# Running W2 and Wo of three chunks as eight 32x64 lanes that also carry the next chunk's attention

## The chip, the cores and the metric

The kernel runs on one core of one Trainium2 chip. The metric is the device time of one execution in microseconds (us). Matrix products run on TensorE (PE), which takes a weight load and a matmul as two instructions; VectorE (DVE), ScalarE (ACT) and GpSimd (POOL) do the elementwise work, and the sequencers of SyncE (SP) and ScalarE issue the DMAs. Each engine works through its own list of instructions in order; semaphores tie the lists together.

## The reference

For 2048 tokens of width 576, in bf16:

```python
xn  = layernorm(x)
out = x + attention(xn, wqkv, wo) + swiglu(xn, w1, w3, w2)

# attention: 32 heads of 18 columns, a causal window of 256 tokens
scores = q @ k.T * 18 ** -0.5
mask   = (i - j >= 0) & (i - j < 256)
o      = softmax(where(mask, scores, -1e9)) @ v
# swiglu: 4608 hidden columns
h      = silu(xn @ w1) * (xn @ w3)
y      = h @ w2
```

## The kernel before

The tokens go through in four **chunks** of 512 (`CH`). A chunk has three stages on PE, one after the other.

**Projection** (`proj_begin`, `proj_end`, `proj_part`; matmuls on line 445): nine items, `("q", 0..3)` and `("8", 7)` for queries and keys and `("v", 0..3)` for values, in the order of `PROJ`. Each item fills a pair of PSUM banks in two halves, and the halves of neighbouring items alternate. DVE and ACT copy queries and keys to SBUF tiles `stage[:, 0..8, :]`. There a head's 18 rows stand at the wrong partitions, so DMAs from SBUF to SBUF move them into `qv` and `kv` (`span_main`, line 512; `span_last`, lines 541 and 543). These DMAs are issued by SP, some by ACT.

**Units** (line 697): 36 units of 18 matmuls (64 rows, 128 columns of weights, 512 tokens streamed; two of them, on the upper and the lower 64 rows, run side by side). A unit makes 128 hidden columns: ACT's tanh (line 706) and two DVE operations (lines 712 and 715) write `hT`. The chunk's attention is threaded between the units, and for later chunks also between the projection's items: `spaced_step` places a **score step** (line 571) when the loop's counter `clock` says so. A score step takes four heads: two 64-row tiles, each with two heads in block-diagonal keys. ACT takes the exponential (line 580), POOL masks (line 607). When all steps of eight heads (`j`, four such groups) are masked, `pv` (line 628) multiplies with the values in eight tiles of 64 rows by 32 columns, and `pv_out`, `o_scale`, `o_turn` and `o_pack` (DVE transposes on lines 637 and 650, reciprocals on 642, a POOL multiplication on 643, DMAs on 654) normalise the result and move it to `oT`. The fourth `pv` comes after the units; its transposes run beside W2.

**W2 and Wo** (`p2_list`, `p2_item`; lines 757, 763, 683): for two halves of 288 output columns, 36 blocks of hidden columns times four token tiles, each a full 128x128 tile with 288 columns streamed; then Wo; DVE adds `x` (line 770) and SP stores the result (line 772). W2's weights come in tiles of four blocks, 288 KB each, into four slots (`load_w2`, line 345); a slot is loaded again when its last use has been placed.

The order of all lists is written out by the loop at the end of the kernel: what it adds first stands first in its engine's list. `_Prog.add` notes who wrote and who read each buffer, and `resolve` turns that into semaphore waits. `job()` hands out three bank pairs in turn for projection items and units, so a unit's matmuls wait until DVE is done with the unit three before it. `load_part` (line 318) brings W1 and W3 in parts of 192 KB.

Of the kernel before, what the change touches and what calls it, by code (L numbers as in the profile page):

```python
# [164 lines left out]
def bass_parallel_sum__sliding_block__glu_gated_swiglu__prompt_kernel(  # L165
# [32 lines left out]
    with ExitStack() as es:  # L198
# [4 lines left out]
        NXP, NOF, NPT, NW13, NW2, NOD = 7, 4, 10, 3, 4, 2  # L203
# [17 lines left out]
        w2 = [sb(f"w2_{i}", [128, 4, HD]) for i in range(NW2)]  # L221
        hT = sb("hT", [128, NF, CH])
        stage = sb("stage", [128, 9, CH])
        qv = sb("qv", [128, G, CH])
        kv = sb("kv", [128, G, NB, 2 * KB])
        kb4 = sb("kb4", [128, G, NV - NB, 2 * KB])
        va = sb("va", [128, NV, G, 2, VW])
# [30 lines left out]
        oT = sb("oT", [128, 5, CH])  # L258
        th = [sb(f"th{i}", [128, CH]) for i in range(2)]
        gs = [sb(f"gs{i}", [128, CH]) for i in range(2)]  # L260
# [77 lines left out]
        def load_w2():  # L338
            nonlocal n2fill
            if n2fill >= NC * 2 * NFC:  # L340
                return
            s = n2fill % NW2
            half, fc = divmod(n2fill % (2 * NFC), NFC)
            n2fill += 1
            add("sp", lambda e: e.dma_start(
                w2[s][:], B_w2[fc * 512:(fc + 1) * 512, half * HD:(half + 1) * HD].rearrange("(fl p) d -> p fl d", p=128)),
                w=[("w2", s)], dma=f"w2_{s}")
# [70 lines left out]
        def pair_of(c, i):  # L418

            return (((0, 1), (2, 3), (8, 4), (5, 6)) if c == 0 else ((8, 0), (1, 2), (3, 4), (5, 6)))[i]  # L420
# [68 lines left out]
        def v_evac(c, tt, b, r, eng):  # L489
            pos = (c * NB + 2 * tt + r) % NV  # L490
            for p in range(2):
                src = PS[64 * r:64 * r + 64, b:b + 2, 0:HD].rearrange("p b (n e d) -> p e b n d", e=2, d=Dh)[:, p, :, :, :]
                dst = va[64 * p:64 * p + 64, pos, :, :, 0:Dh].rearrange("p (b g) n d -> p b (g n) d", b=2)
                kw = {"j" if p else "w": [("va", pos)]}
                if eng == "act":
                    add("act", lambda e, dst=dst, src=src: e.activation(dst, src, ACT.Copy), r=[("ps", b), ("ps", b + 1)], **kw)
                else:
                    add("dve", lambda e, dst=dst, src=src: e.tensor_copy(dst, src), r=[("ps", b), ("ps", b + 1)], **kw)

        def keys_of(a, b, p0, n, p):  # L500
            return kv[p0:p0 + n, a:b, :, KB * p:KB * p + KB].rearrange("q g b f -> q (g b) f")

        SPREAD = 3

        def span_issue(a, b, moves, first, only=slice(None)):
            seen = set()
            for n, (kind, eng, tset, dst, src) in enumerate(moves):
                if n not in range(len(moves))[only]:
                    seen.add(kind)
                    continue  # L510
                keys = [(kind, g) for g in range(a, b)]
                add(eng, lambda e, dst=dst, src=src: e.dma_start(dst, src), r=st_keys(*tset), dma=f"{kind}_{a}",
                    **{"j" if kind in seen or not first else "w": keys})
                seen.add(kind)

        def span_main(a, b, q_eng="sp", only=slice(None)):

            gs_ = list(range(a, b))
            moves = []
            for pr in range(2):  # L520
                moves.append(("q", q_eng, gs_, qv[64 * pr:64 * pr + 2 * Dh, a:b, :], stage[2 * Dh * pr:2 * Dh * (pr + 1), a:b, :]))
            for i in range(3):
                r0 = 4 * Dh + i * Dh
                moves.append(("k", "sp", gs_, keys_of(a, b, 64 * (i // 2) + Dh * (i % 2), Dh, i % 2),
                              stage[r0:r0 + Dh, a:b, :].rearrange("q g (b f) -> q (g b) f", f=KB)))
            span_issue(a, b, moves, True, only)

        def span_last(a, b, only=slice(None)):

            p0 = 64 + Dh  # L530
            order = sorted(range(a, b), key=lambda g: g == SPREAD and a != 2)
            for g in order[only]:
                r0 = (g - (g > SPREAD)) * Dh
                moves = [("k", "sp", [8], keys_of(g, g + 1, p0, Dh, 1),
                          stage[r0:r0 + Dh, 8, :].rearrange("q (b f) -> q b f", f=KB))]
                if g == SPREAD:
                    moves = [("k", "sp", range(9), kv[p0 + r:p0 + r + 2 * 9 - 1:2, g, :, KB:2 * KB], stage[126 + r:127 + r, :, :])
                             for r in range(2)]
                for kind, eng, tset, dst, src in moves:
                    if a == 2:  # L540
                        add(eng, lambda e, dst=dst, src=src: e.dma_start(dst, src), r=st_keys(*tset), j=[("k", g)], dma=f"kl_{g}")
                    else:
                        add(eng, lambda e, dst=dst, src=src: e.dma_start(dst, src), r=st_keys(*tset),
                            j=[("k", x) for x in range(a, b)], dma=f"k_{a}")

        def repack_span(a, b, q_eng="sp"):
            span_main(a, b, q_eng)
            span_last(a, b)

        def keep_keys(g):  # L550
            add("pool", lambda e: e.tensor_copy(
                kb4[:, g, :, :].bitcast(dt.float32), kv[:, g, 2 * NB - NV:NB, :].bitcast(dt.float32)),
                r=[("k", g)], w=[("kp", g)])
# [11 lines left out]
        def scores(c, g, s):  # L565
            col = 0
            for n, (kb, q0, nb) in enumerate(steps_of(c)[s]):
                for r in range(2):
                    r0 = 64 * r
                    out_ = PS[:, SC[r], col * KB:(col + nb) * KB]  # L570
                    add("pe", lambda e, r0=r0, out_=out_, kb=kb, q0=q0, nb=nb: e.matmul(  # L571
                        out_, kb4[r0:r0 + 64, g, kb + NV - NB, :] if kb < 0 else kv[r0:r0 + 64, g, kb, :], qv[r0:r0 + 64, g, q0 * KB:(q0 + nb) * KB],
                        start=True, stop=True, tile_position=(r0, 0)),
                        r=[("kp" if kb < 0 else "k", g), ("q", g)], **{"j" if n else "w": [("ps", SC[r])]})
                col += nb

        def exps(c, g, s, sl):
            pt_of[(c, g, s)] = sl
            w = KB * sum(nb for _, _, nb in steps_of(c)[s])
            add("act", lambda e: e.activation(  # L580
                pt_slot(sl)[:, 0:w, :], PS[:, SC[0]:SC[1] + 1, 0:w].rearrange("p r q -> p q r"), ACT.Exp, scale=scale),
                r=[("ps", b) for b in SC], w=pt_keys(sl))

        def masks(c, g, s):

            at = []
# [8 lines left out]
            sl = pt_of[(c, g, s)]  # L595
# [14 lines left out]
        def pv(c, j, banks):  # L610
# [4 lines left out]
            for s, st in enumerate(steps_of(c)):  # L615
                col = 0
                for kb, q0, nb in st:
                    n += 1
                    pos = (c * NB + kb) % NV
                    for gi in range(2):  # L620
                        g = 2 * j + gi
                        sl = pt_of[(c, g, s)]
                        for pr in range(2):
                            for p in range(2):
# [493 lines left out]
```

## Time and profile before

| | |
|---|---|
| median of 3 runs | 559.48 us (559.39 to 560.43) |
| span of the profiled execution | 557.7 us |
| median less span | 1.8 us |
| PE busy, share of the chain that ended last | 553.1 us (99%), 98% |
| a chunk's period (projection start to projection start) | 137.5 us (142.44 to 279.94 to 417.44) |
| one W2 and Wo stage, chunk 1 | 39.56 us (240.21 to 279.77) |
| a unit of 18 matmuls | 1.94 us |
| ACT, DVE, POOL busy | 259.4, 309.6, 163.3 us |

The profile shows one execution. In its tables of groups, "out<-in" names the tensors, then stands the shape and how often it ran; times are busy us, mean ns of one, and the engine's idle time ahead of it. A timeline row gives the start and the length of a merged run of instructions. An instruction of SP or ACT that issues a DMA is listed under "SPq" or "ACTq", with the time for which that sequencer was held by it; "to landing" is the time from issue to the last of its data.

### The profile page before, as it was taken

To read this page: it belongs to the slowest core of one execution; us is meant where nothing else is said; L and a number is where in the kernel's file an instruction comes from. 1 tells how busy PE (TensorE), PEld (TensorE's weight loads), DVE (VectorE), ACT (ScalarE), POOL (GpSimd) and SP (SyncE) were. 2 spreads that over 40 slices of the span, in tenths; PEclk is the share of its full clock that TensorE was granted. 3 is DMA by queue.
4 is the path that set the end of the run, shared out by engine and by line. 5 is a ranking of instruction groups with operands and counts; after the bars stand their busy time and mean duration, and the time that the engine had idled before them with its cause. 6 is when DMAs were issued, how large, how long until landed. Compare 5 with 4: busy or idle time off the path is not lost.

```text
span 557.7 us, 15727 instructions
## 1 busy us (share of the span) xinstructions
PE 553.1 (99%) x6766; PEld 332.9 (60%) x6766; DVE 309.6 (56%) x578; ACT 259.4 (47%) x357; POOL 163.3 (29%) x389
## 2 busy tenths in 40 slices
PE   8999999999999999999999999999999999999998
PEld 4445545787655455477764554548776555455776
DVE  6465889610365778851056668884105577777211
ACT  6457776100387776500048777650005776765000
POOL 5513454300034445330003444423001343432000
PEclk9999999999999999999999999999999999999999
DMA  9987989978576358466956744966593673562552
GB/s 234 228 177 179 207 141 196 165 201 225 135 139 146 110 139 188 125 144 174 238 107 139 166 115 113 182 153 140 151 249 78 135 172 98 129 142 54 139 149 65
DMA packets 127072, 85.96 MB, mean 154 GB/s; under 512 B 34179, under 2 KB 124763, under 8 KB 127003
## 3 DMA queue, kind: packets, MB, share of 16 engines
q1 hardware_dynamic: 125011, 82.69, 64.5%
q10 hardware_dynamic: 1992, 2.27, 1.7%
q8 instruction: 53, 0.87, 0.7%
q14 instruction: 16, 0.13, 0.1%
HBM read 71.29 MB, written 2.36 MB: 132 GB/s over the span
## 4 chain that ended last, share of the span: by engine, by line
PE 98%; DMA 1%; DVE 0%; ACT 0%; issue 0%; POOL 0%
PE ps L697 50%; PE ps L757 25%; PE ps L445 9%; PE ps L571 6%; PE ps L628 4%; PE ps L763 3%; DMA xp<-in_A_x_dram 1%; PE ps L683 0%; PE ps L390 0%; DVE xn L370 0%; ACT stage L825 0%; ACT xnT L397 0%; DVE stats L353 0%; DVE ofin L770 0%; POOL xn L373 0%
## 5 line engine op out<-in xcount | busy, mean ns | idle before, releaser
L697 PE MATMUL ps<-xnT,w 64*128 64x512 bf16 x1400 | 182.9, 376 | 0.0
L697 PE MATMUL ps<-xnS,w 64*128 64x512 bf16 x1120 | 150.9, 376 | 0.0
L757 PE MATMUL ps<-w,hT 128*128 128x288 bf16 x1152 | 146.6, 286 | 0.0
L712 DVE SCALAR_TENSOR_TENSOR gs<-th,ps 128x512 bf16<-128x512 bf16 x144 | 98.0, 681 | 81.4 <-ACT th L706 80.8
L580 ACT ACTIVATE pt<-ps 128x1024 bf16<-128x1024 f32 (+1 forms) x112 | 113.2, 1010 | 53.5 <-PE ps L571 53.0
L757 PEld LDWEIGHTS ps<-w,hT 128*128 128x128 bf16 x1152 | 112.3, 98 | 29.0 <-issue 0.2
L607 POOL TENSOR_TENSOR pt<-pt,mk 128x128 int32<-128x128 int32 (+1 forms) x199 | 80.8, 428 | 79.2 <-ACT pt L580 79.2
L697 PEld LDWEIGHTS ps<-xnT,w 64*128 64x128 bf16 x1400 | 66.5, 94 | 62.8 <-issue 0.3
L706 ACT ACTIVATE th<-ps 128x512 bf16<-128x512 f32 x144 | 85.5, 594 | 35.3 <-PE ps L697 34.7
L715 DVE SCALAR_TENSOR_TENSOR hT<-gs,ps 128x512 bf16<-128x512 bf16 x144 | 98.9, 687 | 4.9
L697 PEld LDWEIGHTS ps<-xnS,w 64*128 64x128 bf16 x1120 | 53.8, 94 | 54.3
L770 DVE TENSOR_TENSOR ofin<-ps,xp 128x288 bf16<-128x288 f32 x32 | 13.8, 455 | 124.9 <-PE ps L763 66.8
L458 ACT ACTIVATE stage<-ps 128x512 bf16<-128x512 f32 x16 | 9.5, 596 | 142.0 <-PE ps L445 139.7
L607 POOL TENSOR_TENSOR hT<-hT,mk 128x128 int32<-128x128 int32 (+1 forms) x31 | 12.4, 422 | 164.3 <-ACT hT L580 164.3
L571 PE MATMUL ps<-qv,kv 64*128 64x320 bf16 (+4 forms) x528 | 51.5, 260 | 0.0
L571 PEld LDWEIGHTS ps<-qv,kv 64*128 64x128 bf16 x528 | 25.3, 94 | 28.1 <-ACT hT L580 1.7
L445 PE MATMUL ps<-xnT,wp 64*128 64x512 bf16 (+1 forms) x360 | 37.9, 355 | 0.0
L650 DVE STREAM_TRANSPOSE od<-oq 128x256 bf16<-128x256 bf16 x64 | 25.8, 427 | 7.0 <-POOL oq L643 7.0
L580 ACT ACTIVATE stage<-ps 128x1024 bf16<-128x1024 f32 x24 | 24.6, 1024 | 10.2 <-PE ps L571 10.0
L445 PEld LDWEIGHTS ps<-xnT,wp 64*128 64x128 bf16 x360 | 18.9, 94 | 14.5
L643 POOL TENSOR_TENSOR oq<-uq,rden 128x288 bf16<-128x288 f32 x16 | 10.8, 673 | 40.7 <-DVE rden L642 40.7
L445 PE MATMUL ps<-wv,xnT 64*128 64x288 bf16 x288 | 22.2, 283 | 0.1
(75 smaller groups left out, 345.4 us busy)
## 6 DMA issues: line engine op xcount, KB each, us to landing
w<-in_B_w_dram SPq DMA_DIRECT2D x208, 192.0 KB, 4.2
w<-in_B_w_dram SPq DMA_DIRECT2D x72, 288.0 KB, 3.4
xp<-in_A_x_dram SPq DMA_DIRECT2D x30, 144.0 KB, 3.5
out_dram<-ofin SPq DMA_DIRECT2D x32, 72.0 KB, 2.0
xnS<-xnT SPq DMA_DIRECT2D x8, 256.0 KB, 6.6
oT<-od SPq DMA_DIRECT2D x40, 36.0 KB
pt<-in_A_wqkv_dram SPq DMA_DIRECT2D x4, 288.0 KB, 6.8
hT<-in_B_w_dram SPq DMA_DIRECT2D x6, 192.0 KB, 4.2
```

What stands on the lines that cost most here:

```text
L445: op = add("pe", lambda e, out_=out_, st=st, mv=mv, n=n, r0=r0, first=first: e.matmul(out_, st, mv, start=first, stop=(part == 1 and n == ...
L571: add("pe", lambda e, r0=r0, out_=out_, kb=kb, q0=q0, nb=nb: e.matmul(out_, kb4[r0:r0 + 64, g, kb + NV - NB, :] if kb < 0 else kv[r0:r0 + ...
L580: add("act", lambda e: e.activation(pt_slot(sl)[:, 0:w, :], PS[:, SC[0]:SC[1] + 1, 0:w].rearrange("p r q -> p q r"), ACT.Exp, scale=scale) ...
L607: add("pool", lambda e, vb=vb, mm=mm: e.tensor_tensor(vb, vb, mm, ALU.mult), r=(key if n == 0 else []) + ["mk"], **{"w" if n == 0 else "j" ...
L628: add("pe", lambda e, p=p, q=q, pr=pr, sl=sl, g=g, pos=pos, q0=q0, nb=nb, col=col, first=first, n=n: e.matmul(PS[32 * q:32 * q + VW, banks ...
L650: add("dve", lambda e: e.transpose(od[i][:, g % 2, c0:c0 + CH // 2], oq[:, c0:c0 + CH // 2]), r=["oq", "oq0"], **{"j" if half or g % 2 els ...
L697: op = add("pe", lambda e, n=n, r0=r0, r=r, k=k, src=src: e.matmul(PS[:, b0 + r, :], wt[r0:r0 + 64, k, fl * 128:(fl + 1) * 128], src, star ...
L706: add("act", lambda e: e.activation(th[i][:], PS[:, bg, :], ACT.Tanh, scale=0.5), r=[("ps", bg)], w=[("th", i)])
L712: add("dve", lambda e: e.scalar_tensor_tensor(out=gs[i][:], in0=th[i][:], scalar=1.0, in1=PS[:, bg, :], op0=ALU.add, op1=ALU.mult), r=[("t ...
L715: add("dve", lambda e: e.scalar_tensor_tensor(out=hT[:, u, :], in0=gs[i][:], scalar=0.5, in1=PS[:, bu, :], op0=ALU.mult, op1=ALU.mult), r= ...
L757: add("pe", lambda e: e.matmul(bank, hT[:, f, tt * 128:(tt + 1) * 128], w2[sl][:, k, :], start=(f == 0 and half == 1), stop=False), r=[("h ...
L763: add("pe", lambda e: e.matmul(bank, oT[:, k, tt * 128:(tt + 1) * 128], wo[:, k, d0:d0 + HD], start=False, stop=(k == 3 and (half == 0 or ...
```

## The change

**The attention of chunks 1 to 3 moves.** It no longer runs between units: chunk c+1 is projected right after chunk c's units, and its scores and PVs run inside chunk c's W2 and Wo stage. Chunk 0's attention stays between chunk 0's units; chunk 3's W2 stays as it was, apart from the size of the tiles.

**W2 and Wo of chunks 0 to 2 run in eight lanes.** A lane is one of 4 x 2 tiles of 32 rows by 64 columns. For one half, a token tile's 36 blocks are split over four row groups; each group adds into another token tile's bank, and the groups change banks in eight stages (`TURNS`). A stage that takes over a bank waits, through a semaphore (`after`), until the last owner's matmul has ended. A lane has 18 matmuls of W2 in a stage, and Wo's in between.

**Scores take eight heads.** Four lanes do one step of heads (`h2` 0 or 1) while the other four go on with W2. Queries and keys therefore stand at eight places of 18 rows, each on a 32-row border, and are moved there by more DMAs (`spans`). The planner in `w2_lanes` keeps a clock for each lane and writes the matmuls of all lanes, the exponentials, masks, PVs and `events` (loads of W1 and W3, `x`, `xn_swap`, the steps behind a PV) in one order. Scores use two bank pairs in turn.

**W2's tiles** are six blocks (432 KB) in five slots. Their memory also holds chunk 0's keys (`kz`), so chunk 0's tiles are loaded from the hooks of chunk 1's projection.

```diff
-        NXP, NOF, NPT, NW13, NW2, NOD = 7, 4, 10, 3, 4, 2
+        NXP, NOF, NPT, NW13, NW2, NOD = 7, 4, 10, 3, 5, 2
+        FT = 6
-            return (((0, 1), (2, 3), (8, 4), (5, 6)) if c == 0 else ((8, 0), (1, 2), (3, 4), (5, 6)))[i]
+            return (((0, 1), (2, 3), (8, 4), (5, 6)) if c == 0 else ((8, 0), (4, 1), (5, 2), (6, 3)))[i]
...
+        def span(c, kind, hd, half, a, b, eng="sp"):
+            h2, r = divmod(hd, 2)
+            row = 64 * r + 32 * (half ^ h2)
+            rows = slice(row, row + Dh)
...
+            if kind == "q":
+                moves.append((range(a, b), ts, qv[rows, h2, a:b, :], stage[Dh * hd:Dh * hd + Dh, tile_, :]))
+            elif hd < 3:
+                src = stage[4 * Dh + hd * Dh:5 * Dh + hd * Dh, tile_, :]
...
+                    if c % 2 == 0:
+                        moves.append((range(a, b), ts, kq[rows, h2, a:b, 0:2, :].rearrange("q g c f -> q g (c f)"), src))
+                    else:
+                        moves += [(range(a, b), ts, kq[rows, h2, a:b, 2 * x, :], src[:, :, 4 * KB * x:4 * KB * x + 4 * KB]) for x in range(2)]
...
+        def spans(c, a, b):
+            for hd in range(4):
+                for half in range(2):
+                    span(c, "q", hd, half, a, b, "act" if hd > 1 else "sp")
+                for half in range(2):
+                    span(c, "k", hd, half, a, b)
...
+        def score_ops(c, unit, bank):
+            j, h2, s = unit
...
+                            lane = (2 * r + (half ^ h2), half)
+                            rows, at = slice(32 * lane[0], 32 * lane[0] + Dh), (32 * lane[0], 64 * half)
+                            out_, st = PS[64 * half:64 * half + 64, bank[r], cols], kd[rows, h2, j, key_at(c, kb), :]
...
+                                r=[("k", j), ("q", j)], **kw)
...
+        TURNS = ((0, 2, 3, 1), (1, 3, 2, 0), (2, 0, 1, 3), (3, 1, 0, 2))
+        LANES = [(a, b) for a in range(4) for b in range(2)]
...
+        def lane_matmul(c, half, lane, t, k, first, after):
+            a, b = lane
+            rows = slice(32 * a, 32 * a + 32)
+            toks = slice(t * 128 + 64 * b, t * 128 + 64 * b + 64)
...
+                st, mv, keys = hT[rows, i, toks], w2[sl][rows, i % FT, :], [("h", i), ("w2", sl)]
...
+            out_ = PS[64 * b:64 * b + 64, ACC[t], 0:HD]
+            return add("pe", lambda e: e.matmul(
+                out_, st, mv, start=first == "w" or first == "s", stop=False,
+                tile_position=(32 * a, 64 * b), skip_group_check=True),
+                r=keys, after=after, **{"w" if first == "w" else "j": [("ps", ACC[t])]})
...
+                elif head and stage_ != 4:
+                    known = [v[1] for key_, v in ended.items() if key_[:2] == (half, stage_ - 1)]
+                    after = (max(known, key=lambda o: o.pos),)
...
+                if k[0] == "w2":
+                    i = half * NT2 + k[1] // FT
+                    uses[i] = uses.get(i, 0) + 1
+                    if uses[i] == 8 * 4 * FT:
+                        load_w2(c)
+            while events:
+                events.pop(0)[1]()
...
-                    span_main(2, G, "act", slice(2, None))
-                if c == 0 and u == 2:
-                    span_last(2, G, slice(0, 1))
+                    for hd in range(3):
+                        for half in range(2):
+                            span(0, "k", hd, half, 0, 4)
+                if c == 0 and u in (2, 3, 4, 5):
+                    for half in range(2):
+                        span(0, "k", 3, half, u - 2, u - 1)
...
+                if c and u in (25, 27, 29, 31, 33):
+                    load_w2(c)
...
+                hooks = {("q", 2): [lambda: spans(c + 1, 0, 2)], ("8", 7): [lambda: spans(c + 1, 2, 4)]}
+                if c == 0:
...
+                    pv(c, 3, banks)
...
+                    for what in (("q", 0), ("v", 0), ("v", 1), ("v", 2), ("v", 3)):
+                        hooks.setdefault(what, []).append(lambda: load_w2(0, first))
...
+                project(c + 1, hooks)
+                two = (job_ctr - 1) % 3
+                ACC[:] = [*JOBS[(two + 1) % 3], *JOBS[(two + 2) % 3]]
...
+                events = [(3000 + 3200 * i, lambda: parts(1)) for i in range(12)]
...
+                w2_lanes(c, xs, [SC, JOBS[two]], events, put_pv, 1500)
```

## The prediction

> **What bounds the kernel now.** I read the page's busy times and its chain of work first, then the timelines of PE and of SP, then single lines.
>
> ```profile
> PE 553.1 (99%) x6766; PEld 332.9 (60%) x6766; DVE 309.6 (56%) x578; ACT 259.4 (47%) x357; POOL 163.3 (29%) x389
> PE 98%; DMA 1%; DVE 0%; ACT 0%; issue 0%; POOL 0%
> ```
>
> PE is the bound from end to end. So PE time that goes is gained in full, and every wait that PE's list now meets is paid in full. Chunk 2's projection in the timeline of SP's sequencer:
>
> ```profile
> 283.61 2.59 SPq L512 DMA_DIRECT2D kv<-stage  x3
> 286.25 0.77 SPq L543 DMA_DIRECT2D kv<-stage  x1
> 287.12 1.59 SPq L512 DMA_DIRECT2D qv<-stage  x2
> 288.75 2.47 SPq L512 DMA_DIRECT2D kv<-stage  x3
> 291.26 1.59 SPq L543 DMA_DIRECT2D kv<-stage  x2
> 292.89 1.38 SPq L318 DMA_DIRECT2D w<-in_B_w_dram  x2
> ```
>
> Eleven moves of queries and keys follow each other from 283.61 to 292.89: SP is held 0.84 us by each. The line views give the same whatever the size, and a W2 tile holds SP half as long:
>
> ```profile
> L512 SPq DMA_DIRECT2D kv<-stage x33: 781/813/3058, 17.9 to 437.9; - x33
> L543 SPq DMA_DIRECT2D kv<-stage x29: 764/782/1378, 20.6 to 444.3; - x29
> L345 SPq DMA_DIRECT2D w<-in_B_w_dram x18: 368/388/552, 242.4 to 279.1; - x18
> ```
>
> Today these moves are spread: the first score needs six of them, four on SP. That list is what I hold the change against.
>
> **PE's own work, per moved chunk.** A score step costs a unit 0.22 us (a unit start every 1.94 us, 2.16 with a step); 40 steps a chunk are 8.8 us. In lanes a step streams the same 512 columns, but on four of eight lanes: 4.4 us of every lane. That removes 4.4 us. W2 and Wo: 320 matmuls in 39.56 us, 122.5 ns each; a lane has 324 (288 + 32 + 4), so 39.7 us if eight run side by side. The trace has no 32x64 tile. Its nearest row is PV, eight 64x32 tiles:
>
> ```profile
> 53.05 0.32 PE L628 MATMUL ps<-hT,va 64*20 64x320 bf16 x4
> 53.06 0.32 PE L628 MATMUL ps<-pt,va 64*20 64x320 bf16 x4
> 53.19 0.25 PE L628 MATMUL ps<-hT,va 64*20 64x192 bf16 x4
> ```
>
> Eight matmuls of 320 columns take 0.14 us, as one does at the units' rate (512 in 0.216). Upper bound: weight loads come in turn. PV's densest loads are 24 of 20 columns in 0.2 us from 514.67, 8.3 ns each; if that is the price of the columns, 64 cost 27 ns and a round of eight lanes 0.213 us instead of 0.1225: +29 us a chunk. But PV's early groups start eight tiles at once, loads included, so I take 39.7.
>
> The Trainium skill, "TensorE: Matmul & The Clock Gate", section "Wait — 56ns, not 53.3ns?", speaks against the change: matmul starts never come closer than about 25 ns, so eight lanes would need 200 ns a round. By it the three stages would be 75 us longer. The trace does not bear it out: seven PV matmuls of 64 columns start from 53.48 to 53.52.
>
> Handing over banks: a 288-column matmul lasts 286 ns and its slot 122, so its result comes some 0.2 us after the slot's end. Twelve hand-overs are 2.4 us, and between the halves a lane waits for up to four DVE adds of 455 ns, 0.9 on average: 3.3 us, 0 if scores fill them all. I take 3.5 with the lanes' unequal ends before a PV. PVs cost the same in both kernels; switches of tile shape are two a chunk in both. Net −0.9 a chunk, **−2.7 us** for three (ends −13 and +3).
>
> **The key moves.** In the changed order the first score of chunk c+1 stands behind 18 matmuls of each lane, 2.2 us into the lanes, and waits for all queries and keys of the first `spans` call: 14 DMAs on SP for chunk 2, 20 for chunks 1 and 3, plus four on ACT. PE's list is in order, so W2 of all lanes stands behind that score. Time from the projection's start: bare projection 13.0 (13.4 from 142.44 to 155.87, less two steps), lanes from 13.2, score due at 15.4. SP can do the first move early; its second needs item ("q", 2), which PE ends at 7.55 (287.3 less 279.77), plus 0.2 and DVE's 0.69: 8.5. The call's last move is for the next group of heads and isn't needed. Landing takes 2.4 to 3.0 from the issue in oT's rows; I take 2.4.
>
> - Chunk 2: 14 less the first and the last are 12, so the last needed starts at 8.5 + 11 x 0.84 = 17.7 and lands at 20.1: PE waits **4.7**. Behind them SP has the second call (15), then two W1/W3 parts (0.65 each), and only then the load of W2's sixth tile, whose slot the first tile held: issued at 19.4 (the first call's end, 8.5 + 13 x 0.84) + 12.6 + 1.3 = 33.3. A 288 KB tile lands in 3.3 us (3.0 to 6.5); 432 KB I put at 4.0 (3.3 to 5.0, in proportion): 37.3. PE wants it after 88.5 matmuls a lane, 1.2 of scores and 0.7 of hand-overs, lane time 12.7: 20.1 + 10.5 = 30.6. Wait **6.7**.
> - Chunk 3: 18 moves, 8.5 + 17 x 0.84 + 2.4 = 25.2, wait **9.8**; then 24.5 + 21 x 0.84 + 1.3 + 4.0 = 47.4 against 35.7, wait **11.7**.
> - Chunk 1: SP first has four packs of oT behind DVE's last turn (7.7 + 4 x 0.8), a W2 tile, then 20 moves: 28.1. Only then comes the third W2 tile, landing at 32.1, due at lane time 1.5, 14.7: wait **17.4**. The fifth tile stands behind the second call (21 moves): 46.6 + 4.0 = 50.6 against 42.5, **8.1**; the sixth at 52.3 against 51.4, **0.9**.
>
> Together **59.3 us**. At 0.74 us a move it is about 49, at 0.90 about 66.
>
> **Chunk 0's keys.** Before, keys of the first groups were moved at 17.9 to 22.9, and the first score ran at 34.44. Now all of chunk 0's key moves start after unit 1, behind the six W1/W3 parts that end at 28.7. The three long key moves there took 5.7; six shorter ones I put at 6, then three parts (2.1) and two moves (1.7): 38.5, landing 41. Wait **6.5** (4 to 11).
>
> **The fourth PV** used to have W2 as cover. Now the units follow, and DVE's list holds the whole turn of that PV ahead of unit 0: four adds, a transpose, one that waits for the stores of the adds (landing 2.0), then a chain that lasted 4.9 us from 241.85 to 246.76. DVE reaches unit 0 some 6.9 us after PE's end, is done 1.4 later; PE's unit 3 needs the bank at 5.9. Wait 2.4, **7.2 us** for three (0 to 9).
>
> **After a wait** the nearest row is the start, where PE had stood idle: 11 matmuls take 4.11 us, 1.6 more than at their later pace. None of the rows shows PE after another long idle, so 0 to 1.6 each; I take 1.5, by that row, for seven waits over 3 us: **10.5 us**.
>
> Costed at nothing: ACT's 40 exponentials (1.02) are 41 us beside a stage of 53 and more; ACT's eight query DMAs (0.75) delay projection copies, but inside the wait for SP. In units without attention DVE needs 1.37 of 1.94 us, so PE covers it.
>
> **Sum.** 557.7 − 2.7 + 59.3 + 6.5 + 7.2 + 10.5 = 638.5; the median stands 1.8 above this execution's span: **640 us**. Its own range, from the terms' ends, is 600 to 664.
>
> **Rivals.**
> - *The queue is short enough, faster than before.* If SP's moves took 0.28 us or less (chunk 3's 17 steps inside 15.4 − 2.4 − 8.5 = 4.5 us), no score would wait; stores and W2 tiles at 0.36 and 0.39 us come near, 128 partitions each. The change then gives its −2.7 and DVE's turn hides: 557. Against it: no key or query move took under 0.73 us. Chance 0.07.
> - *Only DVE's turn shows:* queue in time, 557 + 7.2 = 564. Chance 0.05.
> - *Half the queue's delay:* later tiles are wanted later, since lanes run slower than I count, and PE does not slow after a wait: 640 − 30 − 10.5 = 600. Chance 0.13.
> - *It doesn't do what it says:* lanes load in turn, 3 x 29 = 88 us more. A lane then reaches each wait later, which takes about 28 off them: 700. For it: the 8.3 ns above; against it: PV's groups. Chance 0.08.
>
> Mine keeps 0.67. The range leaves out the first two and the last, 0.20: **585 to 665**. About 0.2% is what a measurement can tell from no change. Faster by more: 0.06; within: 0.02 (the first rival's upper edge); slower: 0.92.
>
> **What would show it.** Right: in chunks 1 to 3 PE idles some 5 to 17 us a little after the lanes begin, ended by a DMA of kd, qv or W2; SP is issuing without a pause there; a second gap comes near the end of the first Wo; a gap of 2 to 3 us stands at unit 3, ended by DVE. Lane matmuls between the gaps are 122 ns apart per lane. Wrong: no gap at the first score, SP moves well below 0.7 us, or lane rounds of 200 ns.

## The result: 749.75 us, a third slower, and the profile after

| | before | after |
|---|---|---|
| median of 4 runs | 559.95 us (559.39 to 560.59) | 749.75 us (748.21 to 753.15) |
| ratio, 95% interval | | 1.339 (1.336 to 1.343) |
| span of the profiled execution | 557.7 us | 749.5 us |
| mean granted TensorE clock | 1.000 | 0.938 |

The change costs 190 us; 640 had been forecast, with 665 as the upper end. The page of the changed kernel has PE's busy time and its number of instructions, the chain that ended last, the two groups of the lanes, and the row of the queue that brings instructions:

```profile
PE 605.0 (81%) x14134; PEld 376.3 (50%) x14134; DVE 310.7 (41%) x578; ACT 265.5 (35%) x357; POOL 157.8 (21%) x365
...
q8 instruction: 111, 1.82, 1.0%
...
PE 67%; issue 12%; SPq 8%; DVE 4%; DMA 4%; ACT 1%; ACTq 1%; POOL 1%; DVEq 0%
...
L827 PE MATMUL ps<-w2all,hT 32*64 32x288 bf16 x6912 | 179.3, 312 | 82.9 <-issue 58.3
L827 PEld LDWEIGHTS ps<-w2all,hT 32*64 32x64 bf16 x6912 | 136.7, 115 | 110.1 <-issue 74.6
```

PE is idle for 144.5 us of the span (749.5 less 605.0) where it was idle for 4.6. "Issue", which was 0% of the chain, is 12%: time in which PE waited for nothing that the profile shows. And PE has twice the instructions: 14134 matmuls and as many loads, 28268. The queue q8 moved 111 packets of 16 KB. 28268 / 111 is 255; before, 13532 instructions came in 53 packets, 255 as well. By these counts a packet of q8 is a block of 256 PE instructions. In the list of waits of the changed kernel (total us, times, longest us), SP's moves, which I had looked for, come second:

```profile
PE ps L827 <- issue: 66.5, 44, 3.5
PE ps L827 <- DMA w2all<-in_B_w_dram: 22.5, 4, 15.5
PE ps L602 <- issue: 20.4, 11, 4.8
PE ps L658 <- issue: 9.8, 7, 2.2
PE ps L602 <- DMA kd<-stage: 9.8, 2, 7.6
```

Where the time went, by stage, from the starts of the stages in PE's timeline (projection L447, units L730, lanes L827 in the kernel after):

| us | before | after | difference |
|---|---|---|---|
| start and chunk 0's units | 102.7 | 112.3 | +9.6 |
| three projections | 3 x 13.6 | 16.6, 14.4, 14.4 | +5 |
| three W2 and Wo stages | 3 x 39.6 | 121.3, 104.0, 109.7 | +216 |
| units of chunks 1 to 3 | 3 x 84.3 | 71.6, 71.8, 70.8 | −39 |
| last W2 and Wo | 42.5 | 42.5 | 0 |

The units gained what the attention cost them. The lanes, which took that attention over, need 335 us where W2 (119) and attention (39) had needed 157. This is what a lane stage looks like in PE's timeline of the changed kernel (start, length, merged run; in brackets the idle time ahead):

```profile
159.12 0.82 PE L827 MATMUL ps<-w2all,hT 32*64 32x288 bf16 x40 [1.44 <-issue]
...
159.98 1.03 PE L827 MATMUL ps<-w2all,hT 32*64 32x288 bf16 x52
160.75 0.29 PE L602 MATMUL ps<-qv,kd 18*64 18x256 bf16 x4
...
163.12 0.81 PE L827 MATMUL ps<-w2all,hT 32*64 32x288 bf16 x36 [1.87 <-issue]
```

PE works for 2 us, stands for 1.4 or 1.9, works again; one stall ends 4.0 us after the other. Some 45 such stalls of 1 to 2.9 us go through the three stages, and the profile shows nothing that they wait for.

The waits that I had forecast are there too. Chunk 1's third W2 tile in PE's timeline, and the SP sequencer beside it, which issues the tile at 142.54, behind twenty moves:

```profile
128.89 2.03 PE L827 MATMUL ps<-w2all,hT 32*64 32x288 bf16 x96
146.45 1.67 PE L827 MATMUL ps<-w2all,hT 32*64 32x288 bf16 x48 [15.53 <-DMA w2all<-in_B_w_dram]
```

```profile
127.79 3.30 SPq L561 DMA_DIRECT2D kd<-stage  x4
131.13 1.52 SPq L561 DMA_DIRECT2D qv<-stage  x2
132.69 9.81 SPq L561 DMA_DIRECT2D kd<-stage  x12
142.54 1.05 SPq L347 DMA_DIRECT2D w2all<-in_B_w_dram  x2
```

### The profile page after: what moved, and what is told of

Read it like the earlier page. It is cut to its first block, busy times and chain, and to the rows that moved or that the text cites. A ratio compares the mean times of both kernels' runs of the same rounds, so it can differ in the third digit from the quotient of the medians.

```text
span 749.5 us, 30502 instructions
## 1 busy us (share of the span) xinstructions
PE 605.0 (81%) x14134; PEld 376.3 (50%) x14134; DVE 310.7 (41%) x578; ACT 265.5 (35%) x357; POOL 157.8 (21%) x365
## 4 chain that ended last, share of the span: by engine, by line
PE 67%; issue 12%; SPq 8%; DVE 4%; DMA 4%; ACT 1%; ACTq 1%; POOL 1%; DVEq 0%
PE ps L730 33%; PE ps L827 19%; SPq L561 8%; PE ps L796 5%; PE ps L602 3%; PE ps L447 3%; PE ps L658 2%; DMA w2all<-in_B_w_dram 2%; ACTq L561 1%; DVE th L745 1%; DVE hT L748 1%; DVE od L680 1%; DMA out_dram<-ofin 1%; DVE ofin L780 1%; POOL kd L1318 1%
## 5 line engine op out<-in xcount | busy, mean ns | idle before, releaser
L827 PE MATMUL ps<-w2all,hT 32*64 32x288 bf16 x6912 | 179.3, 312 | 82.9 <-issue 58.3
L827 PEld LDWEIGHTS ps<-w2all,hT 32*64 32x64 bf16 x6912 | 136.7, 115 | 110.1 <-issue 74.6
L730 PE MATMUL ps<-xnT,w 64*128 64x512 bf16 x1400 | 180.1, 379 | 4.0 <-DVE hT L748 2.9
L730 PE MATMUL ps<-xnS,w 64*128 64x512 bf16 x1120 | 148.2, 379 | 0.0
L745 DVE SCALAR_TENSOR_TENSOR th<-th,ps 128x512 bf16<-128x512 bf16 x144 | 98.0, 680 | 68.2 <-ACT th L739 68.2
L730 PEld LDWEIGHTS ps<-xnT,w 64*128 64x128 bf16 x1400 | 71.4, 95 | 83.1 <-DVE hT L748 4.3
L748 DVE SCALAR_TENSOR_TENSOR hT<-th,ps 128x512 bf16<-128x512 bf16 x144 | 98.9, 687 | 5.0
L730 PEld LDWEIGHTS ps<-xnS,w 64*128 64x128 bf16 x1120 | 57.5, 95 | 61.5 <-issue 1.1
L602 PE MATMUL ps<-qv,kd 18*64 18x320 bf16 (+4 forms) x1152 | 57.4, 278 | 25.4 <-issue 15.6
L602 PEld LDWEIGHTS ps<-qv,kd 18*64 18x64 bf16 x1152 | 36.0, 115 | 30.2 <-issue 27.6
L447 PE MATMUL ps<-xnT,wp 64*128 64x512 bf16 (+1 forms) x360 | 38.7, 355 | 4.8 <-ACT va L498 3.0
L796 PE MATMUL ps<-w2all,hT 128*128 128x288 bf16 x288 | 36.8, 286 | 0.0
L827 PE MATMUL ps<-wo,oT 32*64 32x288 bf16 x864 | 29.4, 314 | 8.2 <-issue 8.2
L796 PEld LDWEIGHTS ps<-w2all,hT 128*128 128x128 bf16 x288 | 28.0, 98 | 7.5 <-issue 0.5
L639 POOL TENSOR_TENSOR stage<-stage,mk 128x128 int32<-128x128 int32 (+1 forms) x51 | 20.2, 416 | 42.7 <-ACT stage L611 42.6
```

What stands on the lines that cost most here:

```text
L447: op = add("pe", lambda e, out_=out_, st=st, mv=mv, n=n, r0=r0, first=first: e.matmul(out_, st, mv, start=first, stop=(part == 1 and n == ...
L602: return add("pe", lambda e: e.matmul(out_, st, qv[rows, h2, j, mv], start=True, stop=True, tile_position=at, skip_group_check=True), r=[( ...
L639: add("pool", lambda e, vb=vb, mm=mm: e.tensor_tensor(vb, vb, mm, ALU.mult), r=(key if n == 0 else []) + ["mk"], **{"w" if n == 0 else "j" ...
L730: op = add("pe", lambda e, n=n, r0=r0, r=r, k=k, src=src: e.matmul(PS[:, b0 + r, :], wt[r0:r0 + 64, k, fl * 128:(fl + 1) * 128], src, star ...
L745: add("dve", lambda e: e.scalar_tensor_tensor(out=th[i][:], in0=th[i][:], scalar=1.0, in1=PS[:, bg, :], op0=ALU.add, op1=ALU.mult), r=[("t ...
L748: add("dve", lambda e: e.scalar_tensor_tensor(out=hT[:, u, :], in0=th[i][:], scalar=0.5, in1=PS[:, bu, :], op0=ALU.mult, op1=ALU.mult), r= ...
```

## The experiments

The theory formed from that trace (**A**): PE's instructions arrive in blocks of 256, one block in 3.3 to 4.1 us, and a round of eight lanes is 16 instructions in 0.1225 us, 1.96 us a block. The lanes then wait for instructions. Its rivals are named in the expectations. Each kernel was run once, with a run of the kernel before beside it (559.4 to 560.7).

| kernel | us | W2 stages of chunks 0 to 2 |
|---|---|---|
| before | 559.6 | 38.6 each |
| W2 in eight lanes of 32x64 | 651.1 | 67.6, 67.0, 67.9 |
| eight lanes of 64x32 | 655.1 | 68.3, 69.9, 68.3 |
| four lanes of 64x64 | 573.4 | 42.3, 42.2, 39.6 |
| eight lanes, 144 columns | 661.4 | 69.7, 70.0, 68.3 |
| eight lanes, 512 columns | 667.6 | 70.5, 72.4, 72.7 |
| eight lanes, no later W2 loads | 657.4 | 69.1, 67.6, 67.6 |
| a quarter in lanes, spread | 571.4 | 44.3, 39.6, 39.6 |
| the same quarter, bunched | 582.9 | 45.8, 42.8, 45.3 |
| before with twelve idles | 638.1 | 44.1, 54.8, 61.2 (with the idles) |
| after, few moves | 721.5 | 104.4, 96.7, 94.6 (after: 117.3, 101.1, 106.7) |
| after, full tiles | 651.0 | 86.8, 66.9, 78.6 |
| after, full tiles and few moves | 623.3 | 70.2, 69.1, 69.6 |

(The stages here run from the first to the last W2 matmul of the stage.)

### Eight lanes by themselves

```diff
-                add("pe", lambda e: e.matmul(
-                    bank, hT[:, f, tt * 128:(tt + 1) * 128], w2[sl][:, k, :], ...
+                for a in range(128 // 32 ...):
+                    for b in range(128 // 64):
+                        out_ = PS[64 * b:64 * b + 64, ACC[a], 0:HD]
+                        add("pe", lambda e, ...: e.matmul(
+                            out_, hT[rows, f, toks], w2[sl][rows, k, 0:HD], start=False, stop=False,
+                            tile_position=(32 * a, 64 * b), skip_group_check=True), ...
```

> The kernel before, with one thing changed: in chunks 0 to 2 each 128x128 matmul of W2 is issued as eight of 32x64 (four row groups, two column halves, 288 columns each). Row group a always adds into bank a, so no bank is handed over and nothing waits for a neighbour; this mixes the token tiles' sums, so W2's share of those chunks is not the reference's. Attention, key moves and the loads stay as before; Wo keeps full tiles, and its four DVE adds per half no longer overlap W2's end (some 2 us a chunk). 284 matmuls a chunk become 2272, that is 4544 PE instructions with the weight loads, 17.75 blocks of 256. Theory A (instruction supply: in the changed kernel's lane stages one block of 256 PE instructions arrives every 3.3 to 4.1 us, take 3.7): 17.75 x 3.7 = 65.7 us where 284 x 0.1225 = 34.8 us were, +31 a chunk, +93 for three: 650 (635 to 670), with PE gaps of 1 to 2 us about every 3.7 us. Rival B (weight loads of the lanes come in turn, 0.213 us a round): +77, 637, without gaps but with rounds of 0.21 us. Rival C (the lanes themselves cost nothing; the changed kernel lost its time to hand-overs, scores and the key moves): 560 to 566.

651.1 us, A's number. PE's timeline in the first of its lane stages:

```profile
112.87 2.17 PE L767 MATMUL ps<-w,hT 32*64 32x288 bf16 x128 [1.29 <-issue]
117.14 2.93 PE L767 MATMUL ps<-w,hT 32*64 32x288 bf16 x128 [2.11 <-issue]
120.60 2.73 PE L767 MATMUL ps<-w,hT 32*64 32x288 bf16 x128 [0.53 <-issue]
```

Every run of lanes alone has exactly 128 matmuls, with their loads 256 instructions, and an idle stretch ends each. Inside a run every eighth matmul starts 122 to 123 ns after the last, except where the granted clock is half for 3.4 us from 118.4 (the second and third run shown; 240 ns there). So the lanes do run side by side, at just the rate that I had taken. In all, 76.9 us went in 51 waits put down to issue. No score, no hand-over and no new move is in this kernel; none of them is needed for the loss, and rival C falls.

The packets of q8 in this run's trace tie the stalls to the blocks. Each of the 51 waits ends 1.2 to 1.6 us after a packet has landed, and the next packet starts 1.0 us or more (median 1.2) after PE has gone on. A packet takes 1.1 us on average: 1.1 + 1.4 + 1.2 is 3.7 us, the pace of a block.

The Trainium skill, "Runtime: NRT & Kernel Launch", section "Instruction fetch mechanics", describes the same blocks, 16 KiB and 256 instructions, and says that the sequencer fetches the next while it executes the current one and that fetching is hidden because instructions are dispatched more slowly than they come. The first half fits the 128 matmuls of each run; the second does not hold here: dispatch took 7.7 ns an instruction (0.1225 us for 16), supply 14 to 17 (3.5 to 4.3 us for 256).

### The other shape of eight, and four

```diff
-                for a in range(128 // 32 ...):
-                    for b in range(128 // 64):
+                for a in range(128 // 64 ...):
+                    for b in range(128 // 32):        # eight of 64x32; for four of 64x64: 128 // 64
```

> As the run with eight 32x64 lanes, with the other shape of eight: 64 rows by 32 columns of weights, the shape that PV has. The number of instructions is the same, 4544 a chunk, but a weight load is half as wide. (Row group a adds into bank a, so W2's share of chunks 0 to 2 is not the reference's.) Theory A (supply, by the count alone): the same time as the 32x64 lanes, some 650 (635 to 670). Rival B (weight loads in turn, 8.3 ns per 20 columns): 13.3 ns for 32, eight are 0.106 us and fit inside a round of 0.1225: 560 to 566. Rival C: 560 to 566.

655.1 us, with 79.8 us of issue waits. Loads half as wide made nothing faster, so rival B, weight loads in turn, falls. It was also my prediction's fourth rival.

> As the run with eight 32x64 lanes, but four lanes of 64x64: half the instructions, 2272 a chunk, 8.9 blocks of 256. (Row group a adds into bank a, so W2's share of chunks 0 to 2 is not the reference's.) Theory A: 8.9 x 3.7 = 32.9 us, less than the 34.8 that the streaming takes, so nearly no cost: 560 to 572 with small gaps, since the margin is 0.2 us a block. Rival B (loads in turn: 4 x 27 ns = 0.106 us a round): 560 to 566. Rival C: 560 to 566. What it tells is the dose: if time follows the count of instructions, halving them takes away nearly the whole loss of the eight lanes.

573.4 us, 1.4 above A's upper end: 8 instructions a round are 3.92 us a block, which is near the pace of supply; 7.8 us of waits in 11 times are put down to issue. Half the instructions cost 14 us, all of them 92. The loss grows with the shortfall of supply, not in proportion to the count.

### Same instructions, other work; same work, other order

```diff
-                        out_ = PS[64 * b:64 * b + 64, ACC[a], 0:HD]
+                        out_ = PS[64 * b:64 * b + 64, ACC[a], 0:HD // 2]      # and 0:512
```

> The run with eight 32x64 lanes in chunks 0 to 2, but each lane matmul streams 144 columns instead of 288; the other half of W2's columns is left out there (and row group a adds into bank a), so W2's share of those chunks is not the reference's. The count of instructions is the same, 17.9 blocks a stage; the streaming is halved, from 34.8 to 17.4 us a chunk. Theory A (time is 17.9 blocks by 3.7 to 3.8 us): the stage stays at 67 us and the run at 651 (643 to 656). Rival I (a lane matmul has a price of its own beside its columns, a loss of 0.107 us a round): 0.061 + 0.107 = 0.168 us a round, 48 us a stage: 593. Rival J (the loss goes with the streaming): half of it, 0.115 us a round: 548.

> The run with eight 32x64 lanes in chunks 0 to 2, but each lane matmul streams 512 columns of the tile instead of 288 (with row group a adding into bank a, so W2's share of those chunks is not the reference's). Eight full matmuls a chunk open the banks in their whole width, 1.7 us a chunk. The count of instructions is that of the 288- and 144-column runs, 17.9 blocks a stage, and the streaming is 284 x 0.216 = 61.3 us a chunk instead of 34.8. Theory A (a block takes the longer of its streaming, 3.46 us, and its supply, 3.7 to 3.8 us): stages of 67 to 70 us and some 659 (650 to 668), although each matmul now does 1.8 times the work; with issue gaps of a few tenths of a us. Rival I (0.107 us more for every round of lanes, whatever it streams): 0.323 us a round, 92 us a stage: 735. Rival M (lanes in themselves are free and nothing is supplied late at this rate): 644.

144, 288 and 512 columns give stages of 69, 67.5 and 72 us: 3.6 times the streaming, and 4% more time. Rivals I and J fall (593 and 548 against 661; 735 against 668), and so does M (644). The stages of the wider one are 0.5 to 2.7 us above the 67 to 70 that I expected: its block streams for 3.46 us and took 4.0. Why the two do not overlap in full stays open. With 144 columns the run ended 5 us above A's range. Its granted clock is 0.86, and 0.57 to 0.60 in the lane stages: PE was busy for 57% of such a stage and ran mostly at half pace, 120 ns a round instead of some 67. Inside the lanes that cost nothing, since a round's instructions take longer to come, but the Wo matmuls behind a half then started 240 ns apart instead of 122, some 2 us each time. In PE's timelines, 144 columns first, then 512:

```profile
113.20 2.14 PE L767 MATMUL ps<-w,hT 32*64 32x144 bf16 x128 [1.86 <-issue]
```

```profile
117.36 10.84 PE L774 MATMUL ps<-w,hT 32*64 32x512 bf16 x384 [1.17 <-issue]
128.54 7.11 PE L774 MATMUL ps<-w,hT 32*64 32x512 bf16 x256 [0.34 <-issue]
```

At 512 columns two and three blocks pass without a stall: supply and streaming are nearly even.

```diff
+                in_lanes = c + 1 < NC and (f % 8 < 2 and (half == 0 or f > 1))      # spread
+                in_lanes = c + 1 < NC and (half == 0 and 9 <= f < 27)               # bunched
+                if not in_lanes:
```

> The kernel before with a quarter of W2 in eight 32x64 lanes, spread out: in chunks 0 to 2 two of every eight blocks of hidden columns (72 of 288 matmuls a chunk) go in lanes, so 128 lane instructions stand between stretches of 48 instructions of full tiles. (Row group a adds into bank a, so W2's share of those chunks is not the reference's; Wo and its adds come after all of W2 in each half, some 1 to 2 us a chunk.) 176 instructions then last 3.92 us, 256 last 5.7 us, more than the 3.7 us in which a block is supplied. Theory A (supply over a block): the lanes cost nothing but the change of tile shape; 564 (560 to 570), hardly any gap put down to issue. Rival E (every lane instruction has its price wherever it stands; the run with all 284 in lanes lost 91.5 us, 0.107 us for each group of eight): 216 groups, +23: 583.

> The same instructions as in the spread run, in another order: the 72 matmuls a chunk that go in lanes stand together (blocks 9 to 26 of the first half), 1152 lane instructions in a row, 4.5 blocks of 256. (Row group a adds into bank a, so W2's share of chunks 0 to 2 is not the reference's.) Theory A: the stretch streams in 8.8 us and is supplied in 4.5 x 3.7 = 16.7 us, less what the fetch has ahead (one to two blocks): 4 to 8 us lost a chunk, 12 to 23 in all: 578 (572 to 586), with issue gaps inside the stretch only. Rival E (price per instruction): 583, like the spread run. The two runs together decide: A wants them some 10 to 20 us apart, E the same.

571.4 and 582.9 us: the same instructions, in another order, differ by 11.5 us. Rival E, a price per instruction, wanted both at 583; the bunched run lies there, the spread run does not. Bunched, 16.9 us in 11 waits are put down to issue; spread, one wait of 2.7 us. PE's timeline of each, spread first:

```profile
251.60 1.19 PE L768 MATMUL ps<-w,hT 32*64 32x288 bf16 x64
252.72 3.11 PE L760 MATMUL ps<-w,hT 128*128 128x288 bf16 x24
255.77 1.19 PE L768 MATMUL ps<-w,hT 32*64 32x288 bf16 x64
```

```profile
256.73 1.40 PE L768 MATMUL ps<-w,hT 32*64 32x288 bf16 x79
259.66 2.17 PE L768 MATMUL ps<-w,hT 32*64 32x288 bf16 x128 [1.52 <-issue]
263.38 2.17 PE L768 MATMUL ps<-w,hT 32*64 32x288 bf16 x128 [1.56 <-issue]
```

The spread run is 1.4 us above A's range. Its period of 64 lane and 24 full matmuls is 4.17 us where streaming is 3.92 (32 slots of 0.1225), so a change of tile shape costs some 0.12 us, 6.5 us in 54 changes.

### Is it the other traffic?

```diff
+            if n2fill >= NW2:
+                n2fill += 1
+                return
```

> The run with eight 32x64 lanes in chunks 0 to 2, with W2 loaded only into its four slots once; later tiles are left out and the old ones used again, so W2's share is not the reference's. The lane stages then move little data besides the instructions. Question: is the 3.7 us of a block made by other transfers? Theory A (a block's fetch takes its time by itself, one after the other): stages of 67 us and 651 (645 to 655). Rival K (the 288 KB tiles hold the fetch up): the closest two blocks in any run are 3.2 us apart; at that pace 17.9 x 3.2 = 57 us a stage: 622 or less.

657.4 us, stages as before and 79.8 us of issue waits. Rival K falls; A's upper end was missed by 2 us. The W2 tiles do not make the pace of a block; W1, W3 and `x` were still loaded. The packets lie as in the first run: each of the 51 waits ends 1.2 to 1.6 us after a landing. What the 1.4 us behind a landing and the 1.2 us ahead of the next packet are for stays open.

### The moves in SP's queue

```diff
         def span(c, kind, hd, half, a, b, eng="sp"):
+            if c and hd:
+                return
```

> The changed kernel with most key and query moves of chunks 1 to 3 left out: only those of the first of the four heads of a tile are made (6 instead of 20 on SP in a call for chunks 1 and 3, 4 instead of 14 for chunk 2, none on ACT); the other heads' places keep zeros or chunk 0's values, so attention of chunks 1 to 3 is not the reference's. POOL clears the keys' memory at the start, up to 3 us. Theory A (the moves hold SP 0.84 us each, and the waits for them and for the W2 tiles behind them, 36 us in the changed kernel's trace, come on top of the lanes' supply): all of these go but some 4 us at chunk 1's third W2 tile, about 32 us, and with them most of the slow stretches behind the waits (2 to 4 us each, five or six waits, part of it hidden by the supply): 704 (692 to 718). Rival F (the supply is the bound there anyway, and what a wait costs is given back since blocks are fetched meanwhile): 730 to 750. Rival G (the moves' packets slow the instruction fetch as well): below 690, with fetches closer together than 3.3 us.

721.5 us, 28.3 less than the changed kernel; A's range ended at 718, rival F began at 730. The lane stages got shorter by 12.9, 4.4 and 12.1 us, 29.4 together. In the changed kernel the gaps at the scores and tiles that wait for moves are 15.5, 0.6 and 0.7 in chunk 1, 2.2 and 3.5 in chunk 2, 7.6 and 5.6 in chunk 3, 35.8 us; a gap of 4.5 at chunk 1's W2 tile was left here. So some 31 us of these waits went. But PE's idle time in the three lane stages fell by 17.4 us only (121.8 to 104.4), because the lanes' stalls on issue grew:

```profile
PE ps L829 <- issue: 78.0, 53, 2.9
```

That row was 66.5 in 44 before. The other 12.0 of the 29.4 us are PE's busy time: the granted clock of these stages rose from 0.84, 0.88 and 0.90 to 0.90, 0.95 and 0.96. So nearly half of what the waits cost came back as waits for instructions, as rival F says, and the slow stretches behind them came off about as A says. Chunks 2 and 3 now show the lanes' own time: 96.7 and 94.6 us for 6534 PE instructions, 25.5 blocks, 3.75 us a block.

### The lanes undone, the rest kept

```diff
-                w2_lanes(c, xs, [SC, JOBS[two]], events, put_pv, 1500)
+                wo_rest(c, 0, True, False)
+                w2_full(c, xs, [SC, JOBS[two]], events, put_pv, 1500)
```

`w2_full` places the items of `p2_list` and between them the score steps one at a time, and the PVs. (In this order an output sum can overwrite memory that a PV's later steps still read, so attention's values are not the reference's; the next run places the sums behind those steps.)

> The changed kernel with only the lanes undone: W2 and Wo of chunks 0 to 2 are full 128x128 tiles again (576 matmul instructions less their loads a chunk instead of 2304), and the eight-head scores and the PVs of the next chunk are placed between them, one step about every 1.1 us. Key layout, key moves, projection order, W2 tiles and loads stay as changed. PE's streaming work is that of the kernel before within a few us. Theory A (lanes lose by supply, some 100 to 140 us; the rest is the moves in SP's queue, the cold clock and chunk 0's keys): 600 (585 to 625), with the gaps at the first score and the third W2 tile of chunk 1 still there, 15 us or more. Rival C (the waits for moves and hand-overs between lanes carry the loss, not the instructions): the moves are the same, so at least 660. Rival D (the lanes carry all of it and the moves hide): 557 to 565.

651.0 us, 26 above A's range, below rival C's 660 and far above rival D's 565. The lanes are worth 99 us of the change, close to the 91.5 that they cost alone. The expected waits are there, but more is left than I counted. PE's timeline:

```profile
144.71 0.64 PE L602 MATMUL ps<-qv,kd 18*64 18x320 bf16 x8 [11.63 <-DMA kd<-stage]
...
146.20 2.10 PE L796 MATMUL ps<-w2all,hT 128*128 128x288 bf16 x8
...
157.39 0.91 PE L796 MATMUL ps<-w2all,hT 128*128 128x288 bf16 x6
158.23 0.41 PE L602 MATMUL ps<-qv,kd 18*64 18x256 bf16 x8
158.57 1.03 PE L796 MATMUL ps<-w2all,hT 128*128 128x288 bf16 x7
```

A step holds PE for 0.34 us (158.23 to 158.57) where a step between units had cost 0.22. The six matmuls ahead of it take 0.84 (157.39 to 158.23) where their slots are 0.735: the last slot is 0.22 long. So each of the two changes of tile shape costs about 0.11, a step 0.22. The 120 steps are 27 us that I had expected, as "within a few us", to be nothing. And eight matmuls take 2.10 us behind the wait of 11.6.

> The changed kernel with both undone: W2 and Wo in full tiles with the eight-head steps between them (as in the run that undid the lanes, 651), and only the key and query moves of the first of a tile's four heads (so attention of chunks 1 to 3 is not the reference's; POOL clears the keys' memory at the start). The output sums also follow a PV's last steps instead of cutting in. Theory A (lanes and moves are two separate costs): of the waits in the full-tile run, 11.6 us at chunk 1's first score falls to 4 or 5 (a W2 tile instead), 7.6 in chunk 3 and 2.4 in chunk 2 go, and two or three slow stretches of 2 to 4 us with them: 627 (615 to 637). What then stays above 560 is 0.13 us more for each of 120 steps that run alone (16 us), chunk 0's keys (5 us and a slow stretch) and DVE's turns. Rival L (the moves cost nothing of their own once the lanes are gone; the full-tile run's loss is something else): 645 to 651.

623.3 us: the moves cost 27.7 us here (the other place of the output sums included) and 28.3 with lanes; the lanes cost 98.8 us with the moves and 98.2 without. Rival L falls; lanes and moves are two separate costs. What is left above the kernel before is 64 us: 21.8 of PE idle (5.2 at chunk 0's first score, 9.6 in three waits behind a PV's DVE work), four slow stretches of 5 to 10 us, and the lone steps. Counting half of each slow stretch (13 us) and the 27 for lone steps, all but some 2 us of it are found. No version tried beats the kernel before.

### What an idle costs behind itself

```diff
+                if n in (50, 130, 240):
+                    idle_pe(IDLES[c][(50, 130, 240).index(n)])
```

> The kernel before with twelve idles of PE put into W2 (three a chunk, 7 us or more of full tiles behind each): PE waits for a row of 2, 3, 4, 5, 6, 7, 8, 10, 12, 14, 17 and 20 POOL multiplications of 128x128, 0.43 us each, on data that nothing else uses. Idles of about 1.2, 1.6, 2.0, 2.4, 2.9, 3.3, 3.7, 4.6, 5.4, 6.3, 7.5 and 8.8 us, 50 in all. Question: what does an idle cost beyond itself? Theory A (as the gaps of the changed kernel show it: none up to 2.4 us, and behind the longer ones PE runs at half pace for 5 to 9 us): 2.5 to 4.7 us each for eight, 28 more: 638 (628 to 652). The prediction's 1.5 us for each over 3 us: 10 more, 620. Rival H (slow stretches belong to lanes and small tiles, not to idles): 610, no 250 ns matmuls behind the idles.

638.1 us. The idles were 1.1, 1.7, 2.2, 2.7, 3.3, 3.8, 4.3, 5.4, 6.5, 7.5, 9.1 and 10.7 us, 58.3 in all; the run is 20.2 us longer than that explains. After 2.2 us and less PE went on at its pace. From 2.7 us on it ran at half pace for 3.0 to 6.0 us behind the idle, which cost 1.4 to 2.9 us each time and 17.6 for the nine, 2.0 on average. Of the rest 2 us come from the counting: an idle is counted from the end of the last matmul, 0.17 us behind its slot. PE's timeline, 80 matmuls behind an idle of 1.1 us and behind one of 2.7, then four of Wo behind one of 3.3 (0.65 us at full pace):

```profile
110.91 9.97 PE L767 MATMUL ps<-w,hT 128*128 128x288 bf16 x80 [1.12 <-POOL scr L752]
...
255.60 11.64 PE L767 MATMUL ps<-w,hT 128*128 128x288 bf16 x80 [2.73 <-POOL scr L752]
270.50 0.62 PE L767 MATMUL ps<-w,hT 128*128 128x288 bf16 x2 [3.26 <-POOL scr L752]
270.92 1.17 PE L774 MATMUL ps<-wo,oT 128*128 128x288 bf16 x4
```

The forecast's 1.5 us was somewhat too small, my later 2.5 to 4.7 too large, and rival H falls. The total agreed with A only because the idles themselves were 8 us longer than planned.

## Why the prediction was wrong

The direction and the named waits were right; the time was 110 us short of the result, outside the range. The step that failed is the first term, PE's own work in the lanes. Term by term, in the prediction's order:

- **PE's work, −2.7: wrong, about +130.** The matmul rate in it was right: rounds of 122 ns, eight at a time, in the changed kernel's sort of lane by itself. The step went on from "a lane has 324 matmuls" to "39.7 us" without asking where 16 instructions a round come from. A stage has 25.5 blocks; at the 3.75 us of the run with few moves (3.77 in the run of eight lanes by themselves) that is 96 us, three are 287, and W2 and attention before had 157. Undoing the lanes alone gave 98 to 99 us back, though the full tiles in their place paid 27 for lone score steps. The upper end that I gave this term, +3, did not hold it, and the rival with slower lanes (700) had another mechanism, which the 64x32 lanes refuted. My test for it, "lane rounds of 200 ns", could not have shown it: between the stalls the rounds are as I said.
- **Could the profile before have told?** In part. Its page has 53 blocks on q8, and the closest two in its trace start 4.0 us apart. A lane stage has 25.5 blocks for the 52 us or so that the prediction gave it, 2.0 us for each. Nothing in the trace shows blocks at that pace. That does not prove a limit, but it is a bound that the prediction could have drawn and did not.
- **Key moves, 59.3: right in kind and place, too large.** Gaps of 15.5, 0.6, 0.7 (chunk 1), 2.2, 3.5 (chunk 2), 7.6 and 5.6 (chunk 3) stand where I had 17.4, 8.1, 0.9, 4.7, 6.7, 9.8 and 11.7. The 3.5 is only in part one of them: the profile puts it down to issue, and to a W2 tile only the last 0.4. The first of each chunk is some 2 us shorter, in part because the projections took 1 to 3 us longer than I counted. The later ones are much shorter, since the slow lanes came to their tiles later; that much the third rival had said, without the reason. Without most moves 28.3 us went.
- **Chunk 0's keys, 6.5:** 4.8.
- **The fourth PV's turn, 7.2:** 2.9 us in three waits of PE for hT, the longest 1.7 where I had 2.4.
- **Slow PE after waits, 10.5:** right in kind, too small for one wait. The changed kernel has five gaps over 3 us, not seven; behind them the granted clock is half for 4.2 to 6.0 us, 24.8 in all, half of which is 12.4. In stages that wait for instructions part of that is hidden, as in the run with 144 columns, where a low clock cost little; shorter gaps have slow stretches too. So this is a rough size.
- **Left out:** projections are 5 us longer, 4.8 of it waits for the copies of values, 3.0 on ACT and 1.8 on DVE. In the run with few moves, where ACT has no query moves after chunk 0, the 3.0 is gone and the 1.8 is still there. I had costed ACT's moves at nothing.

The measured terms, 130 + 36 + 5 + 3 + 12 + 5, give 191 for the 191.8 us between the spans. They overlap: leaving out some 31 of the 36 us took only 17.4 us of PE's idle time away. So close an agreement is luck.

## What to carry to other kernels

Count instructions as you count columns: a split into smaller tiles keeps the streaming and multiplies the list, and here PE got one block of 256 in 3.5 to 4.3 us, 14 to 17 ns an instruction, in any stretch of more than a block or two. Read the instruction queue's row and the closest blocks in the trace before you halve a tile; bursts of half a block among large tiles were free but for the change of shape. Count waits beside that: what stands in a sequencer's queue ahead of a load, and some 2 us more for each idle of 2.7 us and over among full tiles. In a stage that waits for instructions, part of such a wait is given back.

## What the runs showed of the hardware

- **The supply of instructions has a pace of its own.** In the run of eight 32x64 lanes full runs of 128 matmuls start 3.46, 3.73, 4.01 or 4.28 us after one another, each within 0.02 us and with nothing between: steps of 0.27 us. So do those of 144 columns; with no later W2 loads the values are the same but for three at 4.56. The next packet of q8 starts only after PE has taken up the block before (1.0 us or more later at all 51 stalls).
- **Matmuls of different tiles can start 8 ns apart.** With 144 columns at full clock a round of eight took mostly 62 to 67 ns. The Trainium skill, "TensorE: Matmul & The Clock Gate", section "Wait — 56ns, not 53.3ns?", has starts never closer than about 25 ns; that does not hold for the tiles side by side here.
- **The clock follows idleness.** In the run with twelve idles those of 2.2 us and less cost nothing behind them, those of 2.7 and more did. The Trainium skill, "TensorE: Matmul & The Clock Gate", section "Part 1: The HAM clock gate (the "warmup" mystery)", has the clock low after an idle window of about 3.4 us; the idle of 2.7 us shows that less can do it. Other kernels show slow stretches behind still shorter gaps (2.4 us in the run with full tiles and few moves, then 10 us slow), so the gap's length alone does not decide it. In the traces a stretch of half clock inside a kernel lasts 3.41 us or a multiple of it, up to 34.1 with 144 columns.
- **A change of tile shape costs about 0.12 us** between lanes on 32-row borders and 128x128: 0.25 us for two changes in the spread run, 0.22 for the two around a lone score step.
